# Taking the last 64 tokens of two batches through the first attention together, with tail outputs on 128x32 tiles

## The chip, the cores and the metric

The kernel runs on one core of one Trainium2 chip. The metric is the device time of one execution in microseconds (us), the median of several runs. A core has a matrix engine (PE, with its weight loads shown as PEld), a vector engine (DVE), a scalar engine (ACT), GpSimd (POOL) and a sync engine (SP) that issues DMAs. Each works through its own list of instructions in order; semaphores tie the lists together. Matmul results land in PSUM, which has eight banks of 512 fp32 columns on 128 partitions, and only DVE and ACT copy them out. DMAs issued from POOL, SP and ACT all move data between device memory and the core's SBUF.

## The reference

There are 8 batches of 576 tokens. The first stage is an attention with 8 heads of width 64, whose keys and values are averaged over groups of 8 tokens, so each head has 72 keys:

```python
k_p = k.reshape(B, H, Sp, pool, D).mean(axis=3)
v_p = v.reshape(B, H, Sp, pool, D).mean(axis=3)
scores = scale * np.matmul(q, k_p.transpose(0, 1, 3, 2))
attn = np.exp(scores - max); attn = attn / (attn.sum(-1) + 1e-09)
x = np.matmul(attn, v_p)          # heads side by side: B x S x 512
```

The second stage is a causal attention of width 64 in each of 4 experts; a gate keeps the best two experts of each token and weighs their outputs:

```python
logits = x @ w_gate               # top 2 of 4, softmax over the two
for e in range(E):
    q = x @ wq[e]; k = x @ wk[e]; v = x @ wv[e]
    a = softmax(causal(scale * (q @ k.transpose(0, 2, 1))))
    ye = a @ v @ wo[e]
    out += weight_of_expert_e * ye
```

## The kernel before, in words

576 tokens are four blocks of 128 and a tail of 64. The four blocks are the main part of a batch (512 columns). The tails of an even batch and the odd one after it share one block of 128: `place(b, 4)` is block 4 of a tile that holds both batches, and `half(b)` says which 64 partitions belong to which.

Nothing in the kernel is scheduled by the compiler. One long string, `SEQ`, lists all steps as tokens, and a loop at the end issues them one by one, so that the instructions of each engine stand in the string's order. A token reads: name, arguments, batch, then `@` and PSUM bank, then `d` for a copy on DVE instead of ACT, or `p` where a store is issued by a token of its own. `S12:3@4` is step S with arguments 1 and 2 for batch 3 into banks 4 and 5. Tokens with a capital letter are matmul groups on PE (H are idle matmuls at the start); the small letter of the same name is what empties the bank.

For each batch the steps are:

- `L`: loads of q (four quarters of 144 KB), k and v (576 KB each), issued on POOL's queue in the string's order and cast to bf16 on the way. q, k and v each have three buffers.
- `PK`, `kc`, `kt`: pool the keys and turn them; `PV`, `vc`: pool the values; `u`: turn q in 32x32 blocks.
- `E` and `e`: scores of the first attention and their exponential (`Es`, `es`). The argument is the head group 0 or 1 for the main part, and 2 for the tail of both groups.
- `D`, `d`, `x`: sums over the keys, then a logarithm and an exponential that give the reciprocals (`Dn`, `dn`, `dx`); `O`, `o`: outputs times reciprocals into the tile xT (`Ov`, `ov`). Again 2 is the tail.
- `P`, `p`: projections to the experts' queries and keys, `P_t` for the tail; `V`, `v`: values and gate logits; `g`: the gate.
- `S`, `s`, `a`: scores of the second attention, their exponential, the causal mask on POOL. `S03` is the tail's block against itself.
- `B`, then `bz`, `bg`, `b`: outputs of the second attention and their scaling. The last argument is the part: 0 and 1 for two blocks each, 2 for the tails of both batches (`B02`, `B12`: experts 0 and 1, and 2 and 3).
- `T`, `t` or `F`: the transpose before the last projection, through PE or by a DMA of SP; `Y`, `y`: last projection and copy, `z`: the store. `Y4` is the block of both tails, `ya` and `yb` the two halves of its copy in the last batch.

PE sees its 128x128 array in different shapes: E works on strips of 32 rows and 128 columns, S on 64 rows, the groups PK, PV, D and O on columns of 32, `B02` and `B12` on columns of 64, everything else on the whole array. Nearly all matmuls are issued by one helper, `mm` at line 226, so a view by line shows them all as L226; they are told apart by the tiles that they read.

The steps that the change touches are `Es`, `es` (line 336), `heads`, `Dn`, `part`, `Ov`, `ov` (lines 373 and 382), `P`, `p`, `Sb`, `sb` (lines 491 and 497), `am` and `Bv`, and the whole of `SEQ`. The second attention of a batch needs its tail's queries early: every score tile but the first reaches to token 576.

Of the kernel before, what the change touches and what calls it, by code (L numbers as in the profile page):

```python
# [8 lines left out]
FP32 = mybir.dt.float32  # L9
# [14 lines left out]
def kernel(  # L24
# [36 lines left out]
    LONG = (0,)  # L61
    HALF = TPP // 2
# [23 lines left out]
    etas = bufs(2, [KR, H, S], BF16, "eta")  # L86
    rzas = bufs(2, [128, 2, S], FP32, "rza")
# [4 lines left out]
    qks = bufs(2, [128, 2, NEP, SPAD], BF16, "qk")  # L92
# [6 lines left out]
    warm = const.tile([128, 512], BF16, name="warm")  # L99
    ident = const.tile([128, 128], BF16, name="ident")  # L100
    diff = const.tile([128, 128], FP32, name="diff")
# [151 lines left out]


# [56 lines left out]

    def four(pairs):
        return [pairs[0], pairs[0] + 1, pairs[1], pairs[1] + 1]

    def Es(b, pairs, g):
        banks = four(pairs)
        for j, cols, o in pieces(b, g):
            for par in range(2):
                for i in range(4):
                    rows = slice(32 * i, 32 * i + 32)  # L320
                    mm(psum[:, banks[i], o : o + cols.stop - cols.start],
                       kpTs[b % 2][rows, 2 * j + par].rearrange("p c j -> p (c j)"),
                       qTs[b % 2][rows, j, cols, par], start=(par == 0), stop=(par == 1))

    def es(b, pairs, dve, g, half):
# [4 lines left out]
        if len(got) == 2:  # L330
            dst = etas[b % 2][:, :, cols].rearrange(by, g=2)[:, 2 * half : 2 * half + 2]
# [4 lines left out]
        nc.scalar.activation(out=dst, in_=src, func=EXP, scale=ATT_EXP_SCALE)  # L336

    def heads(b, g, cols):
        for i in range(4):
            yield i, 4 * g + i, etas[b % 2][:, 4 * g + i, cols]  # L340
# [7 lines left out]
    def part(t, b, g):  # L348
        got = pieces(b, g)
# [12 lines left out]
    def Ov(b, bank, g, t):  # L362
        got = pieces(b, g)
# [107 lines left out]
    def Sb(b, bank, ep, ti):  # L471

        off = 0
        for i in range(NEP) if ti == 3 else [ep]:
            for c, c0, c1 in STILES[ti]:
                k0 = 128 * c - (64 if c == 4 and b % 2 else 0)
                for e in range(2):
                    r0 = e * HD
                    mm(psum[:, bank + e, off : off + c1 - c0],
                       qks[b % 2][r0 : r0 + HD, 1, i, k0 : k0 + 128],  # L480
                       qks[b % 2][r0 : r0 + HD, 0, i, c0:c1])
                off += c1 - c0

    def sb(b, bank, dve, ep, ti):
# [4 lines left out]
        if ti == 3:  # L489
            for e in range(2):  # L490
                nc.scalar.activation(
                    out=et[half(b), :, e, eo : eo + n],
                    in_=psum[half(b), bank + e, 0 : 2 * n].rearrange("p (a n) -> p a n", a=NEP),
# [8 lines left out]
    def am(b, ep, ti):  # L502
        et = etbs[b % 2]
        if ti == 3:
            blk = et[half(b), :, :, EOFF[4] : EOFF[4] + 64]
            nc.gpsimd.affine_select(
                out=blk, in_=blk, pattern=[[0, NEP], [0, 2], [1, 64]], compare_op=ISGE,
                fill=0.0, base=0, channel_multiplier=-1,
            )
# [108 lines left out]
    def z(b, c, queue):  # L618
# [16 lines left out]
        u00:0 r1:0d w1:0 u01:0 PK0:0@0 W0:0 kc0:0 PK1:0@0 W1:0 kt0:0d kc1:0 u10:0 L_k:1 E0:0@24 H1:0@1 u11:0 H1:0@0  # L635
        H1:0@0 H1:0@0 e00:0 kt1:0 e01:0 c1:0d E1:0@02 e11:0 H1:0@6 H1:0@6 H1:0@4 H1:0@5 e10:0 E2:0@46 PV:0@2 e20:0
        L_q3:1 e21:0 D2:0@3 D0:0@6 H1:0@7 D1:0@7 vc:0 O20:0@2 O01:0@4 d0:0 O00:0@6 c0:0d O11:0@5 x0:0 d1:0 x1:0 d2:0
        O10:0@0 H1:0@1 H1:0@1 c3:0 o00:0 H1:0@7 o01:0 L_q2:1 H1:0@1 o10:0 X0:0@6 o11:0 X1:0 X2:0 X3:0 c2:0 x2:0 o20:0
        P_k1:0@2 P_k0:0@3 P_t0:0@5 PK:1@4 p_k1:0 p_k0:0 W3:0 h0:0d L_q1:1 N:0 L_q0:1 W2:0 p_t0:0d S00:0@2 H1:0@6 H1:0@5
        S02:0@6 kc:1 L_v:1 S03:0@4 s00:0 S01:0@0 s02:0 H1:0@2 kt:1d s03:0 u1:1 H1:0@3 u0:1 E1:1@46 s01:0 L_k:2 E0:1@02  # L640
        c4:0d e10:1 e01:1 V2:0@4 v2:0d L_q0:2 a00:0 e11:1 V1:0@5 V3:0@2 V0:0@4 v1:0d D1:1@5 L_q3:2 v3:0d v0:0d L_q1:2
        PV:1@3 a02:0 e00:1 E2:1@06 D0:1@4 d1:1 L_q2:2 g0:0 vc:1d x1:1 H1:0@5 O10:1@5 o10:1 L_v:2 O11:1@3 d0:1 g1:0 g2:0
        o11:1 e20:1 x0:1 O01:1@2 O00:1@4 S12:0@0 B01:0@5 o01:1 e21:1 D2:1@3 s12:0 d2:1 PK:2@6 a01:0 g3:0 O20:1@7 o00:1
        bz01:0 S10:0@0 L_k:3 g4:0 x2:1 g5:0 g6:0 S11:0@2 P_q0:1@4 kc:2 g7:0 o20:1 s10:0 g8:0 P_q1:1@6 kt:2d L_q0:3 a12:0
        p_q0:1d V0:1@7 L_q3:3 s11:0 u1:2 p_q1:1 a11:0 P_t0:1@4 g9:0 bg01:0 L_q2:4 v0:1d a03:0 E1:2@02 p_t0:1 L_q1:3
        b01:0 u0:2 e10:2 V2:1@6 v2:1d a10:0 P_k0:1@7 p_k0:1d e11:2 E0:2@04 B11:0@6 B10:0@2 L_q2:3 L_k:4 B00:0@7 bz10:0
        e01:2 e00:2 bz11:0 PV:2@3 bz00:0 bg11:0 D1:2@4 b11:0 bg00:0 bg10:0 d1:2 P_k1:1@5 b00:0 vc:2d E2:2@06 b10:0
        D0:2@4 x1:2 e21:2 L_v:3 O11:2@3 L_q0:4 O10:2@2 p_k1:1d PK:3@6 d0:2 o11:2 O01:2@7 S03:1@4 kc:3 e20:2 x0:2 o01:2
        S01:1@0 L_q1:4 o10:2 V3:1@3 L_q3:4 s03:1 s01:1 V4:1@6 v3:1 S10:1@4 O00:2@7 S00:1@0 v4:1d s10:1 S11:1@2 s00:1
        V1:1@6 T00:0@4 L_v:4 o00:2 P_q0:2@5 s11:1 kt:3d t00:0d v1:1d S02:1@0 a03:1 u0:3 s02:1 p_q0:2d S12:1@6 P_q1:2@4  # L650
        E0:3@02 g1:1 g2:1 g3:1 g0:1 a00:1 V2:2@5 s12:1 u1:3 g4:1 g5:1 p_q1:2d P_k1:2@6 e01:3 v2:2d E2:3@24 g6:1 P_k0:2@7
        L_q0:5 e20:3 L_q3:5 a02:1 p_k1:2d e21:3 T10:0@6 t10:0d g7:1 g8:1 E1:3@24 p_k0:2d B12:1@6 g9:1 e00:3 PK:4@0 e11:3
        PV:3@1 a10:1 bz12:1 bg12:1 S00:2@4 kc:4 e10:3 a12:1 b12:1 vc:3d B02:1@7 D1:3@6 bz02:1 u0:4 D0:3@0 B01:1@1
        T11:0@2 a11:1 W4:0 V3:2@3 s00:2 bz01:1 D2:2@4 bg02:1 d0:3 D2:3@0 t11:0d O01:3@5 bg01:1 O11:3@2 d1:3 L_k:5 x0:3
        d2:3 O10:3@6 b02:1 x1:3 b01:1 v3:2d d2:2 B10:1@1 o01:3 kt:4 T01:0@7 t01:0 L_q1:5 V1:2@0 v1:2 V0:2@3 v0:2 O00:3@5
        PV:4@4 x2:2 o10:3 O20:2@0 o11:3 o00:3 L_q2:5 u1:4 E0:4@26 vc:4 x2:3 L_q2:6 P_k1:3@5 P_q1:3@4 bz10:1 bg10:1 e01:4
        o20:2 g1:2 b10:1 p_q1:3d E1:4@06 e00:4 Y1:0@2 p_k1:3d y1:0dp L_v:5 V2:3@4 v2:3d Y3:0@3 L_q1:6 e11:4 Y2:0@5 g2:2
        P_t0:2@2 y3:0dp e10:4 y2:0p L_k:6 a01:1 p_t0:2d g0:2 E2:4@06 D0:4@4 e21:4 O20:3@5 L_q0:6 d0:4 o20:3 g3:2 O01:4@3
        PK:5@2 D1:4@6 L_v:6 S12:2@4 P_k0:3@7 e20:4 x0:4 kc:5 s12:2 S10:2@0 d1:4 o01:4 S11:2@2 S02:2@4 s10:2 p_k0:3d
        V4:3@6 kt:5d s11:2 B11:1@7 T02:1@0 P_q0:3@1 s02:2 T12:1@2 u1:5 p_q0:3 t02:1d bz11:1 V1:3@3 u0:5 P_t0:3@0 x1:4  # L660
        L_q3:7 p_t0:3 O00:4@4 v4:3d bg11:1 v1:3d L_q3:6 g4:2 D2:4@1 L_q0:7 L_q2:7 PV:5@6 b11:1 O10:4@7 t12:1d a00:2
        O11:4@5 d2:4 o00:4 vc:5 E2:5@02 e21:5 V3:3@4 g5:2 o10:4 S03:2@6 o11:4 S01:2@2 e20:5 s03:2 s01:2 S01:3@0 v3:3d
        B00:1@5 bz00:1 T10:1@6 x2:4 g6:2 t10:1d P_k0:4@4 a01:2 bg00:1 s01:3 E0:5@26 b00:1 e01:5 V0:3@5 T11:1@0 p_k0:4d
        a12:2 t11:1d P_k1:4@4 e00:5 E1:5@06 e11:5 v0:3d B00:2@5 bz00:2 p_k1:4d Y4:1@2 e10:5 g7:2 P_q0:4@3 T01:1@4 g8:2
        y4:1dp g1:3 a02:2 g9:2 S11:3@6 PK:6@2 p_q0:4d bg00:2 b00:2 O20:4@0 kc:6 g2:3 O01:5@1 t01:1 s11:3 a01:3 D0:5@3
        d0:5 PV:6@4 L_v:7 O11:5@5 o20:4 O00:5@6 g3:3 g4:3 g0:3 D1:5@2 x0:5 vc:6d D2:5@0 zs2:0 d1:5 a10:2 O10:5@3 o01:5
# [121 lines left out]
```

## Time and profile before

| | us |
|---|---|
| median of three runs | 156.86 (156.32 to 157.36) |
| the profiled execution, its own time | 154.86 |
| its span, first to last instruction | 153.1 |
| PE busy | 140.8 (92%) |
| ACT busy | 131.0 (86%) |
| DVE busy | 116.0 (76%) |
| POOL busy | 91.5 (60%) |

The granted PE clock is 0.984 of full speed over the span. Busy times of a stage say little by themselves: the engines work on several batches at once, and PE's matmuls are pipelined. Read where each engine waits, and for what. In the rows of the profile a line gives start and length in us, engine, source line, operation, what is written and read, the shape, and how often; in square brackets stands how long the engine was idle before it and what ended that.

### The profile page before, as it was taken

The numbers are of one execution on the slowest core, as the hardware profiler recorded it, in microseconds if no ns is written. First come the engines' busy times: TensorE is split into PE (matmuls) and PEld (weight loads), VectorE is DVE, ScalarE is ACT, GpSimd is POOL, SyncE is SP. The second block draws the span as 40 slices with busy tenths as digits, with TensorE's granted clock in tenths as the row PEclk, the third lists the DMA queues.
The fourth block names the chain that finished last, engine by engine and source line by source line (L and its number), as shares of the span: only waits on it lengthen the run. The fifth ranks groups of instructions, "written<-read, shape, count | busy, mean of one in ns | idle before, by whom it ended". The sixth has DMA issues, their size and how long they took to land.

```text
span 153.1 us, 5376 instructions
## 1 busy us (share of the span) xinstructions
PE 140.8 (92%) x2118; PEld 75.7 (49%) x2118; DVE 116.0 (76%) x341; ACT 131.0 (86%) x235; POOL 91.5 (60%) x211
## 2 busy tenths in 40 slices
PE   6778996999999999999999999999999999999920
PEld 2223452555553555556545666744545656656410
DVE  1871785698899599889879979897785866798440
ACT  3359759998999899999999999999999999887910
POOL 6995449689776896983469544440752655682000
PEclk9999999999999999999999999999999999999985
DMA  4999999999999999999999993166250027899976
GB/s 126 235 188 181 183 177 182 182 180 184 181 182 183 180 183 184 180 185 246 182 178 117 234 153 43 39 72 180 92 197 2 4 49 72 279 354 370 345 285 196
DMA packets 68282, 26.67 MB, mean 174 GB/s; under 512 B 62112, under 2 KB 63392, under 8 KB 68256
## 3 DMA queue, kind: packets, MB, share of 16 engines
q0 software_dynamic: 56928, 14.72, 96.8%
q1 hardware_dynamic: 10960, 10.88, 23.5%
q10 hardware_dynamic: 368, 0.72, 1.6%
q8 instruction: 16, 0.26, 0.7%
q14 instruction: 10, 0.08, 0.1%
HBM read 30.42 MB, written 9.44 MB: 260 GB/s over the span
## 4 chain that ended last, share of the span: by engine, by line
PE 70%; DMA 12%; ACT 8%; POOL 3%; DVE 2%; issue 1%; DVEq 0%; POOLq 0%
PE psum L226 69%; DMA qraw<-in_q_dram 7%; DMA vraw<-in_v_dram 5%; ACT etb L497 3%; ACT eta L336 3%; POOL kraw L133 2%; PE psum L235 1%; ACT rza L359 1%; POOL qraw L133 1%; ACT rza L355 1%; DVE qT L303 1%; ACT vaug L217 0%; DVE otail L567 0%; DVE kf L283 0%; DVE ofin L217 0%
## 5 line engine op out<-in xcount | busy, mean ns | idle before, releaser
L497 ACT ACTIVATE etb<-psum 128x1024 bf16<-128x1024 f32 x48 | 47.0, 1030 | 1.4 <-PE psum L226 1.1
L336 ACT ACTIVATE eta<-psum 96x1024 bf16<-96x1024 f32 (+1 forms) x48 | 36.3, 807 | 3.5 <-PE psum L226 3.2
L514 POOL TENSOR_SCALAR_AFFINE_SELECT etb<-etb 128x256 bf16<-128x256 bf16 x64 | 24.9, 409 | 13.5 <-ACT etb L497 13.4
L133 POOL DMA_DIRECT2D qraw<-in_q_dram x30 | 20.0, 674 | 5.3 <-DMA vraw<-in_v_dram 3.6
L382 DVE TENSOR_TENSOR xT<-psum,rza 128x512 bf16<-128x512 f32 x32 | 20.5, 681 | 1.6 <-ACT rza L359 0.8
L226 PE MATMUL psum<-wvg,xT 128*128 128x260 bf16 x144 | 20.0, 274 | 0.4 <-ACT eta L336 0.4
L226 PE MATMUL psum<-xT,wqp 128*128 128x64 bf16 (+1 forms) x128 | 19.5, 286 | 0.0
L226 PE MATMUL psum<-wop,oT 128*128 128x512 bf16 (+1 forms) x74 | 19.2, 374 | 0.3 <-DVE oT L217 0.3
L226 PE MATMUL psum<-xT,wkp 128*128 128x512 bf16 (+1 forms) x128 | 19.3, 286 | 0.0
L226 PEld LDWEIGHTS <-etb 128*128 128x128 bf16 (+1 forms) x480 | 14.9, 102 | 7.3 <-issue 4.5
L217 DVE CAST qk<-psum 128x512 bf16<-128x512 f32 (+2 forms) x26 | 16.3, 638 | 2.6 <-PE psum L226 2.3
L226 PE MATMUL psum<-vaug,etb 128*128 128x65 bf16 (+1 forms) x480 | 17.4, 195 | 0.0
L226 PE MATMUL psum<-qk 64*128 64x64 bf16 (+4 forms) x192 | 16.0, 276 | 0.2
L226 PEld LDWEIGHTS <-xT 128*128 128x128 bf16 x144 | 12.9, 97 | 6.3 <-issue 2.7
L217 DVE COPY ofin<-psum 128x512 f32<-128x512 f32 (+1 forms) x18 | 11.9, 669 | 3.4 <-PE psum L226 3.3
L303 DVE STREAM_TRANSPOSE qT<-qraw 128x576 f32<-128x576 f32 (+1 forms) x18 | 13.4, 753 | 0.9 <-DMA qraw<-in_q_dram 0.8
L133 POOL DMA_DIRECT2D kraw<-in_k_dram x11 | 11.5, 1051 | 4.3 <-DMA kraw<-in_k_dram 3.4
L567 DVE TENSOR_TENSOR osc<-psum,gt 128x256 bf16<-128x256 f32 x32 | 13.4, 421 | 0.6
L226 PE MATMUL psum<-qT,kpT 32*128 32x64 bf16 (+1 forms) x256 | 12.4, 289 | 1.4 <-DVE qT L303 1.3
L217 ACT COPY ofin<-psum 128x512 f32<-128x512 f32 (+1 forms) x19 | 10.4, 579 | 3.6 <-PE psum L226 3.3
L226 PE MATMUL psum<-eta,vp 96*32 96x64 bf16 (+1 forms) x256 | 12.9, 287 | 0.0
L359 ACT ACTIVATE rza<-rza 128x512 f32<-128x512 f32 (+1 forms) x24 | 12.6, 529 | 0.1
(81 smaller groups left out, 216.8 us busy)
## 6 DMA issues: line engine op xcount, KB each, us to landing
out_dram<-ofin SPq DMA_DIRECT2D x32, 256.0 KB, 3.2
vraw<-in_v_dram POOLq DMA_DIRECT2D x8, 576.0 KB, 11.8
qraw<-in_q_dram POOLq DMA_DIRECT2D x30, 144.0 KB, 9.8
kraw<-in_k_dram POOLq DMA_DIRECT2D x7, 576.0 KB, 10.7
out_dram<-ofin SPq DMA_DIRECT2D x7, 128.0 KB, 3.6
xT<-in_q_dram ACTq DMA_DIRECT2D x2, 288.0 KB, 4.6
xT<-in_k_dram SPq DMA_DIRECT2D x2, 192.0 KB, 4.9
kraw<-in_k_dram POOLq DMA_DIRECT2D x4, 96.0 KB, 5.1
```

What stands on the lines that cost most here:

```text
L133: nc.gpsimd.dma_start(out=dst, in_=src)
L217: (nc.vector.tensor_copy if dve else nc.scalar.copy)(out=out, in_=in_)
L226: nc.tensor.matmul(out=out, lhsT=lhsT, rhs=rhs, start=start, stop=stop)
L235: nc.tensor.transpose(out=out[s], in_=in_[:, s], identity=ident[0:n, 0:n])
L303: nc.vector.transpose(out=dst.rearrange("p (a s n) -> p a n s", s=32, n=n)[:, :, own], in_=src.rearrange("p (a n d) -> p a n d", n=n, d=32 ...
L336: nc.scalar.activation(out=dst, in_=src, func=EXP, scale=ATT_EXP_SCALE)
L355: nc.scalar.activation(out=rz, in_=z, func=LN)
L359: nc.scalar.activation(out=rz, in_=rz, func=EXP, scale=-1.0)
L382: nc.vector.tensor_tensor(out=xT[:, 2 * got[0][0] + t : 2 * got[-1][0] + t + 1 : 2, m + got[0][1].start : m + got[0][1].stop], in0=psum[:, ...
L497: nc.scalar.activation(out=et[:, ep, :, eo : eo + n], in_=psum[:, bank : bank + 2, 0:n], func=EXP, scale=MOE_EXP_SCALE,)
L514: nc.gpsimd.affine_select(out=blk, in_=blk, pattern=[[0, 2], [1, 128]], compare_op=ISGE, fill=0.0, base=0, channel_multiplier=-1,)
L567: nc.vector.tensor_tensor(out=osc(b, ep, part).rearrange("p c (e d) -> p e c d", e=2), in0=o[:, :, :, 0:HD], in1=gt.to_broadcast([128, 2, ...
```

## The change

From batch 2 on, the tails of an even batch and of the odd batch after it pass the first attention together, when the odd batch is at its turn: `PAIRED = (3, 5, 7)`. The tokens `E2`, `e2`, `D2`, `d2`, `x2`, `O2`, `o2`, `P_t`, `p_t`, `S03`, `s03` and `a03` of batches 2, 4 and 6 are gone, and those of 3, 5 and 7 work on both tails. Batches 0 and 1 keep their own. The tails' exponentials and reciprocals get tiles of their own; the tile for the idle matmuls and one for constants move into them.

`sb` for the tails makes one call per batch over both experts of a pair of banks in place of two. `Bv` for the tails writes pieces of 32 tokens in place of 64, with twice as many matmuls on 128x32 tiles. The whole string is ordered anew: PE has 2206 matmuls in place of 2118, ACT 204 instructions in place of 235, DVE 346 in place of 341. Some copies change between ACT and DVE, banks are given out anew, the loads stand in another order, and the store of the last block (`zs4:7`) becomes a token at the very end.

```diff
+    PAIRED = (3, 5, 7)
-    etas = bufs(2, [KR, H, S], BF16, "eta")
-    rzas = bufs(2, [128, 2, S], FP32, "rza")
+    etas = bufs(2, [KR, H, MAIN], BF16, "eta")
+    eta_ends = bufs(2, [128, H, 2 * TAIL], BF16, "etaT")
+    etaTs = [t[0:KR] for t in eta_ends]
+    rzas = bufs(2, [128, 2, MAIN], FP32, "rza")
+    rzaT = const.tile([128, 2, 2 * TAIL], FP32, name="rzaT")
...
+    def tails(b):
+        return (b - 1, b) if b in PAIRED else (b,)
+    def ends(b):
+        n = len(tails(b))
+        return [(j, bb, TAIL * m, TAIL * (n * j + m)) for j in range(2) for m, bb in enumerate(tails(b))]
...
     def Dn(b, bank, g):
+        if g == 2 and b in PAIRED:
+            for h in range(H):
+                mm(psum[32 * (h % 4) : 32 * (h % 4) + 32, bank, 2 * TAIL * (h // 4) : 2 * TAIL * (h // 4) + 2 * TAIL],
+                   onesd[:, :], etaTs[b // 2 % 2][:, h, :])
+            return
...
-        cols, n = (tcols(b), TAIL) if nm == "t" else (mcols(b), MAIN)
+        cols, n = (tail_cols(b), TAIL * len(tails(b))) if nm == "t" else (mcols(b), MAIN)
...
-            for e in range(2):
+            for m, bb in enumerate(tails(b)):
                 nc.scalar.activation(
-                    out=et[half(b), :, e, eo : eo + n],
-                    in_=psum[half(b), bank + e, 0 : 2 * n].rearrange("p (a n) -> p a n", a=NEP),
+                    out=etbs[bb % 2][half(bb), :, :, eo : eo + n].rearrange("p a e n -> p e a n"),
+                    in_=psum[half(bb), bank : bank + 2, 2 * n * m : 2 * n * m + 2 * n].rearrange(
+                        "p e (a n) -> p e a n", a=NEP),
                     func=EXP, scale=MOE_EXP_SCALE,
                 )
...
                     for h in range(2):
-                        mm(av(b, bank, part)[64 * h : 64 * h + 64, e, 0, :],
-                           etbs[h][:, ep, e, col : col + TAIL],
-                           vaugs[b // 2 % 2][:, place(h, c), 2 * ep + e, :], start=(c == 0), stop=(c == NTC - 1))
+                        for x in range(0, TAIL, 32):
+                            mm(av(b, bank, part)[64 * h + x : 64 * h + x + 32, e, 0, :],
+                               etbs[h][:, ep, e, col + x : col + x + 32],
+                               vaugs[b // 2 % 2][:, place(h, c), 2 * ep + e, :], start=(c == 0), stop=(c == NTC - 1))
...
-        Y2:7@2 B12:7@0 bz12:7 B02:7@4 bg12:7 bz02:7 b12:7 T12:7@5 bg02:7 b02:7 T02:7@0 t12:7d t02:7d Y4:7@4 zs3:6 y2:6p
-        y1:7p y0:7p y3:7p y2:7p zs2:6 zs1:7 zs0:7 ya4:7 yb4:7d zs3:7 zs2:7
+        zs1:4 T01:7@5 y0:7dp a03:7 t01:7d T11:7@2 t11:7d B02:7@1 zs0:4 bz02:7 bg02:7 B12:7@0 bz12:7 Y3:7@2 y2:6p b02:7
+        Y2:7@5 T02:7@1 bg12:7 b12:7 y1:6p t02:7d y1:7p y3:7p zs0:6 zs3:6 zs2:6 zs1:6 zs0:7 zs1:7 y2:7p T12:7@4 zs3:7
+        t12:7d Y4:7@0 ya4:7dp yb4:7p zs2:7 zs4:7
```

The loads of batches 3 to 5 stand in the string in these orders, with a quarter of q as q and a digit for the batch:

```
before: k3 q3 q3 q4 q3 q3 k4 v3 q4 q4 q4 v4 q5 q5 wo k5 q5 q5 q6 v5
after:  k3 q3 q3 q3 q3 q4 q4 q4 q4 k4 wo v3 k5 v4 q5 q5 q5 q5 v5
```

More of the change, by code (lines that the diff above doesn't have):

```diff
@@ L91 @@
     etbs = bufs(2, [128, NEP, 2, ECOLS], BF16, "etb")
-    qks = bufs(2, [128, 2, NEP, SPAD], BF16, "qk")
+    qk_all = const.tile([128, 2, 2, NEP, SPAD], BF16, name="qk")
+    qks = [qk_all[:, i] for i in range(2)]
     vaugs = bufs(2, [128, NPC, E, HD + 1], BF16, "vaug")
@@ L362, in Ov @@
     def Ov(b, bank, g, t):
+        if g == 2 and b in PAIRED:
+            for h in range(H):
+                for u in range(2):
+                    for j, bb, m, _ in ends(b):
+                        if j == h // 4:
+                            o = 4 * TAIL * j + 2 * TAIL * u + m
+                            mm(psum[32 * (h % 4) : 32 * (h % 4) + 32, bank, o : o + TAIL],
+                               vps[bb % 2][:, h, u::2], etaTs[b // 2 % 2][:, h, m : m + TAIL])
+            return
         got = pieces(b, g)
@@ L504, in am @@
         if ti == 3:
[L505 to L509, printed above, removed]
+            for bb in tails(b):
+                blk = etbs[bb % 2][half(bb), :, :, EOFF[4] : EOFF[4] + 64]
+                nc.gpsimd.affine_select(
+                    out=blk, in_=blk, pattern=[[0, NEP], [0, 2], [1, 64]], compare_op=ISGE,
+                    fill=0.0, base=0, channel_multiplier=-1,
+                )
             return
@@ L649 @@
[L649 to L653, printed above, removed]
```

175 lines of the change are left out of this document (96 added, 79 removed).

## The prediction

> **What bounds the kernel now.** I read the page first, for which engine is full and where.
>
> ```profile
> span 153.1 us, 5376 instructions
> PE 140.8 (92%) x2118; PEld 75.7 (49%) x2118; DVE 116.0 (76%) x341; ACT 131.0 (86%) x235; POOL 91.5 (60%) x211
> PE   6778996999999999999999999999999999999920
> PEclk9999999999999999999999999999999999999985
> DMA  4999999999999999999999993166250027899976
> ```
>
> PE is at nine tenths from the eighth slice to the last but two. The DMA engines are full through the first 24 slices (some 95 us), then free, then full again at the end with the output. ACT is nearly as full as PE, so which of the two bounds has to be settled. For that I read the sums by stretch:
>
> ```profile
> core 0: us, PE busy (x) PEld busy (x) DVE busy (x) ACT busy (x) POOL busy (x), PEclk, DMA share, GB/s
> 25.00:60.00 35.00, 34.32 (x569) 18.09 (x565) 29.70 (x83) 33.30 (x61) 28.38 (x58) 1.00 1.80 182
> 60.00:100.00 40.00, 40.00 (x690) 23.12 (x688) 34.98 (x102) 39.27 (x73) 24.67 (x58) 1.00 1.36 155
> 100.00:144.50 44.50, 44.39 (x584) 25.08 (x584) 34.82 (x111) 41.53 (x76) 20.74 (x69) 1.00 0.57 165
> ```
>
> Both look full, and a busy PE here may be matmuls whose modelled ends overlap a wait. So I go to the timeline of PE alone and take differences of starts, which no modelled end can blur:
>
> ```profile
> 52.20 0.63 PE L226 MATMUL psum<-qT,kpT 32*128 32x512 bf16 x8
> 52.76 0.51 PE L226 MATMUL psum<-vaug,etb 128*64 128x65 bf16 x20
> 53.20 0.52 PE L226 MATMUL psum<-kraw,poolk 96*32 96x128 bf16 x24
> ...
> 62.54 0.60 PE L226 MATMUL psum<-wop,oT 128*128 128x512 bf16 x2
> 62.98 0.61 PE L226 MATMUL psum<-wvg,xT 128*128 128x260 bf16 x4
> 63.43 1.02 PE L226 MATMUL psum<-wop,oT 128*128 128x512 bf16 x4
> 64.29 0.40 PE L226 MATMUL psum<-xT,wqp 128*128 128x64 bf16 x8
> ...
> 65.30 0.51 PE L226 MATMUL psum<-eta,vp 96*32 96x64 bf16 x20
> 65.64 0.51 PE L226 MATMUL psum<-kraw,poolk 96*32 96x128 bf16 x24
> ```
>
> Two matmuls of 512 columns take 62.98 - 62.54 = 0.44 us, so 0.22 each; four of 260 columns 0.45, so 0.11 each; four more of 512 columns 0.86, again 0.22. That is columns streamed one after the other with nothing between. Eight matmuls on 32-row strips run four at a time, 8 x 0.22 / 4 = 0.43, but the next group starts 0.56 later: 0.13 us go where the shape of the array tile changes. So in the middle PE does not wait; its time is columns streamed plus about 0.13 us for each change of tile shape. What is won there must come out of columns or changes.
>
> At the head PE waits for data, and at the end for the last tail:
>
> ```profile
> 23.71 0.78 DVE L303 STREAM_TRANSPOSE qT<-qraw 128x576 f32<-128x576 f32 x1 [0.84 <-DMA qraw<-in_q_dram]
> 24.55 1.30 PE L226 MATMUL psum<-qT,kpT 32*128 32x512 bf16 x16 [0.88 <-DVE qT L303]
> 26.29 0.94 PE L226 MATMUL psum<-wvg,xT 128*128 128x260 bf16 x7 [0.43 <-ACT eta L336]
> ```
>
> So batch 1 cannot start before its queries land (about 23.6), whatever stands ahead of it; from 24.55 on the time is PE's order.
>
> **The change, part by part.** Everything is a difference against the profiled execution's 154.86 us, whose span is 153.1.
>
> *1. PE's own work.* I counted matmuls and changes of tile shape in the two program orders. The merged P_t of two batches streams 16 x 128 columns in place of 32 x 64. From 64.29, eight 64-column matmuls take about 8 x 0.03 = 0.23 (the row's 0.40 includes the drain of the last), so 0.93 a pair; 16 x 0.22 / 4 = 0.88 after. Three pairs: -0.15 us with the merged denominators. Scores and outputs of the tails keep their count. The eight tail outputs (B02, B12) go from 20 matmuls on 128x64 tiles to 40 on 128x32. From 52.76 to 53.20 the old form takes 0.44 with its change of shape, so 0.31. The new form was never run with 128 rows, but the nearest row is at 65.30: 20 matmuls with 32-column tiles, four of them of 512 columns, take 0.34; 0.22 of it is those four, which leaves 0.12 for 16, four at a time in 0.03. Forty then take 0.30: equal. Bounds: 0.30, and 0.60 if only two ran at a time (+2.4 us over eight); I take 0.30. What the new form does win is neighbours: D, O, PK and PV have the same shape, so no change falls between them. By my count the changes after batch 1's first scores fall from 110 to 108 (of 126 and 122 in all): 2 x 0.13 = -0.26. Changes out of the old 128x64 shape were the dearer ones, for which I add -0.2. Sum -0.6 us, from -0.9 to +1.8.
>
> [...]
>
> *2. ACT.* Merging takes off twelve short exponentials and gives six of double length, and the masks' sources (s03) become one call per batch in place of two.
>
> ```profile
> L336 ACT ACTIVATE eta<-psum 96x1024 bf16<-96x1024 f32 x32 | 31.0, 1023 | 3.0 <-PE psum L226 2.7
> L336 ACT ACTIVATE eta<-psum 96x256 bf16<-96x256 f32 x16 | 5.5, 376 | 0.5 <-PE psum L226 0.5
> L359 ACT ACTIVATE rza<-rza 128x512 f32<-128x512 f32 x16 | 10.2, 635 | 0.1
> L359 ACT ACTIVATE rza<-rza 128x128 f32<-128x128 f32 x8 | 2.6, 319 | 0.0
> L491 ACT ACTIVATE etb<-psum 64x128 bf16<-64x128 f32 x16 | 3.5, 266 | 0.5 <-PE psum L226 0.4
> ```
>
> The 96x512 form stands between its two rows: 0.376 + 0.647 x 256 / 768 = 0.59, so 12 x 0.376 - 6 x 0.59 = 0.97 off. Reciprocals: 0.42 for 256 columns by the same line, 6 x 0.319 - 3 x 0.42 = 0.65 off, and the logarithms before them about as much (0.6). Masks: 16 x 0.266 - 8 x 0.37 = 1.3 off. That is 3.5 us; copies that the new order hands from ACT to DVE take some 2.7 more (counted over the tokens), and DVE gains about 1.1 on balance. Value for the end: 0, since PE's starts above show no wait on ACT in the middle. Bounds: 0 and -5; the latter is a rival.
>
> *3. The loads.* Their order moves, and this costs.
>
> ```profile
> DMA packets 22045, 5.83 MB, mean 182 GB/s; under 512 B 21795, under 2 KB 22038, under 8 KB 22038
> ...
> 60.30 1.19 POOL L133 DMA_DIRECT2D vraw<-in_v_dram  x1 [0.54 <-PE psum L226]
> vraw<-in_v_dram POOLq DMA_DIRECT2D x1, 576.0 KB, 10.8
> 71.62 0.59 PE L226 MATMUL psum<-vraw,poolv 96*32 96x512 bf16 x4
> ```
>
> The first row is the stretch from 28 to 60 us: 5.83 MB in 32 us, so 576 KB need 3.2 and a quarter of q 0.8. The others are batch 5's values: issued at 60.30, landed 10.8 later at 71.1, first used at 71.62, half a microsecond of margin. In the new order one quarter of q less stands ahead of them, so they land about 70.3; but by my sum of streamed columns and changes PE has 2.0 us less to do before it reaches that group, and gets there at 69.6. It waits 0.7. Earlier, batch 4's keys now stand behind three more quarters of q, and the wait would be absorbed in this one. At the head nothing is gained: q of batch 1 is still behind the same 576 KB of k. Value +0.7, bounds 0 and +1.5: the upper one if the stretch from 25 to 37 us, where the row at 26.29 shows PE on ACT's heels, passes its delay on.
>
> *4. The last tail.*
>
> ```profile
> 143.00 1.59 PE L226 MATMUL psum<-wop,oT 128*128 128x512 bf16 x6
> 144.51 0.82 PE L226 MATMUL psum<-vaug,etb 128*64 128x65 bf16 x40
> 145.89 0.23 PE L235 MATMUL psum<-ident,otail 128*128 128x128 bf16 x1 [0.55 <-DVE otail L567]
> 146.28 0.23 PE L235 MATMUL psum<-ident,otail 128*128 128x128 bf16 x1 [0.17 <-DVE otail L567]
> 146.83 0.61 PE L226 MATMUL psum<-wop,oT 128*128 128x256 bf16 x4 [0.32 <-DVE oT L217]
> ...
> 147.48 0.42 DVE L217 COPY ofin<-psum 128x256 f32<-128x256 f32 x1 [0.71 <-PE psum L226]
> 147.97 0.48 SPq L622 DMA_DIRECT2D out_dram<-ofin  x1
> 148.51 1.07 SPq L626 DMA_DIRECT2D out_dram<-ofin  x2
> ```
>
> Before, the two tail outputs stand last, and PE idles 0.55 + 0.17 + 0.32 and more while DVE scales them. In the new order two projections (Y3:7 and Y2:7, each 2 x 0.22) stand between the tail outputs and their transposes. They cover 0.87 of a wait that is at least 1.04; what stays is the hand-over of the last transpose to its copy and on to Y4. I take -0.8; bounds -1.0 and -0.4.
>
> *5. The last stores.* Before, two stores of 256 KB are issued behind the last one's first half, at 148.51 and 0.54 after that; the end at 153.1 is theirs. In the new order the last projection's store is the last, so those two are ahead of it if the queue has come that far. That is 148.51 + 0.54 - 147.97 = 1.1 us less after the last copy; the smaller last store (two halves of 128 KB on two queues) may add 0.1. I take -1.2; bounds -1.6, and +0.5 if the queue is behind.
>
> Sum: -0.6 + 0 + 0.7 - 0.8 - 1.2 = -1.9 us. The profiled execution would take 154.86 - 1.9 = 153.0. The median of the runs shown, 156.86, stands 2.0 above the profiled execution, so the median forecast is **155.0 us**.
>
> **The rivals.**
>
> *ACT is the bound after all.* For it: 39.27 of 40.00 and 41.53 of 44.50 us busy, and a busy PE may be waiting. [...] Against it: the starts 62.54, 62.98, 63.43 and 64.29 leave no room. If it holds, part 2 pays up to 5 of its 6.2 us, of which I allow 2.5 beyond the sum: 152.5.
>
> *The store queue is behind.* The order moves the stores; nine of them then follow each other at the very end, and at 0.54 us each they need 4.9 us. If the queue reaches them 1.5 us late, part 5 turns from -1.2 to +0.3: 156.5, no change. For it: the DMA row is at nine tenths there. Against: the same number of stores leaves the queue over the same stretch before.
>
> *The merged tails starve PE* (the other side). Each merged tail is one serial chain: scores, exponentials, denominators, logarithm, reciprocal, output, multiplication, projection, copy. From a denominator to its output the reciprocal alone is 0.42 and the logarithm as much, 0.84; in the new order about 1.0 us of other PE work lies between them, and each chain occurs three times with two such joints more (multiplication to projection, copy to scores). If every joint is short by 0.6 us, nine joints cost 5.4: 160.4. It decides from 0.4 us a joint on, where 3.6 us would make the kernel over 1% slower. Against: the covers that I counted at the other joints are 1.2 us and more.
>
> *Weight loads follow each other in the tail outputs.* [...] By the trace the bound is two at a time, which was 0.60 in part 1, +2.4 us in all: 157.4. Against: the 16 matmuls at 65.30 have 16 different stationary slices and take 0.12.
>
> **How the numbers follow.** Forecast 53% (154.0 to 156.2), ACT the bound 7%, store queue 20%, starved tails 15%, weight loads 5%. A difference of 1% (1.6 us) is about what a measurement of this kernel can tell from no change. The forecast's own spread reaches over -1%: about 0.43 of its 0.53 is faster, the rest the same. Faster 0.43 + 0.07 = 0.50; the same 0.10 + 0.20 + 0.03 = 0.33; slower 0.17. The range runs from 152.8 (ACT freed in part) to 158.2 (the starved tails from their point of decision, and the weight loads).
>
> **What would show it.** Part 1: a tail output group followed 0.30 to 0.45 us later by the next group; more than 0.6 is the weight-load rival. Part 2: ACT's busy sum near 125 us while PE stays at its full digits. Part 3: batch 5's value pooling waiting for its DMA, and less than a microsecond in all such waits. Parts 4 and 5: under a microsecond of idle PE between the last tail output and Y4, and no store issued after Y4's. The prediction is wrong if PE shows idle time in the middle, or if stores are still being issued two microseconds after the last copy.

## The result, and the profile after

The changed kernel takes **164.27 us** (median of four runs, 162.26 to 164.99); the kernel before took 157.11 in the same comparison (156.32 to 158.71). The ratio is 1.0515, 95% interval 1.0414 to 1.0616. The forecast was 155.0 with a range to 158.2: wrong in sign, and 9.3 us off.

The page of the changed kernel (an execution of 164.99 us, span 163.1) already says where to look. It is the longest of its four runs, and the profiled execution of the kernel before (154.86) is a short one, so the difference of these two, which is taken apart below, is 10.0 us where the medians differ by 7.2.

```profile
span 163.1 us, 5500 instructions
...
PE 145.6 (89%) x2206; PEld 76.6 (47%) x2206; DVE 117.2 (72%) x346; ACT 128.7 (79%) x204; POOL 91.4 (56%) x211
...
PE   6886997999999995999999955999999999999940
...
PEclk9999997799999999999999995599999999999996
DMA  4999999999999999999399990016052224799995
...
q8 instruction: 17, 0.28, 0.7%
```

PE's digits fall to 5 in slice 16 (61 to 65 us) and in slices 24 and 25 (94 to 102 us), and the granted clock falls twice, to 7 and to 5; before, both rows stood at nines in these slices, but for the head. PE has 88 pairs of a weight load and a matmul more than before (2206 against 2118). The last row is the queue that brings instructions; it returns below. The timeline of PE at the two places (start, duration, operation, and in brackets the idle time ahead of it with what ended it):

```profile
59.09 0.85 PE L231 MATMUL psum<-vaug,etb 128*32 128x65 bf16 x80
...
62.94 0.36 PE L231 MATMUL psum<-etaT,vp 96*32 96x64 bf16 x19
65.36 0.24 PE L231 MATMUL psum<-etaT,vp 96*32 96x64 bf16 x5 [2.06 <-issue]
...
94.16 0.49 PE L231 MATMUL psum<-vaug,etb 128*32 128x65 bf16 x40
94.48 0.45 PE L231 MATMUL psum<-etaT,vp 96*32 96x64 bf16 x29
...
95.51 0.53 PE L231 MATMUL psum<-kraw,poolk 96*32 96x128 bf16 x24
95.85 0.38 PE L231 MATMUL psum<-eta,onesd 96*32 96x512 bf16 x1
99.59 1.04 PE L231 MATMUL psum<-eta,onesd 96*32 96x512 bf16 x7 [3.35 <-issue]
```

Both stalls lie **inside** a group of equal matmuls: after 19 of the 32 of O20 of batch 3, and after the first of the four of D1 of batch 6. Their operands were there, or the first ones could not have run. "issue" means that the profile shows nothing that PE waited for. PE's waits summed by what ended them (total, times, longest):

```profile
PE psum L231 <- issue: 5.4, 2, 3.4
PE psum L231 <- DMA vraw<-in_v_dram: 1.3, 1, 1.3
```

The clock, by stretches of 3.41 us on the grid on which it changes (PE busy is the second number, the granted clock the one before the DMA share):

```profile
23.40:26.81 3.41, 2.00 (x22) 0.56 (x19) 2.79 (x6) 3.39 (x5) 2.66 (x5) 1.00 1.89 185
26.81:30.22 3.41, 3.23 (x16) 2.20 (x15) 1.35 (x6) 2.86 (x4) 2.70 (x3) 0.50 1.81 178
...
95.08:98.49 3.41, 1.15 (x69) 0.73 (x63) 1.89 (x7) 1.07 (x2) 0.42 (x2) 1.00 1.04 113
98.49:105.31 6.82, 5.72 (x52) 3.49 (x52) 1.73 (x4) 2.86 (x5) 0.00 (x0) 0.50 0.01 2
```

At half clock two matmuls of 512 columns take 0.84 us (102.29 to 103.13), against 0.44 in the kernel before. If matmuls that keep PE busy for 3.23 us at half clock need half of that at full clock, the first stretch costs an estimated 1.6 us and the second, 5.72 busy, 2.9. The sixteen matmuls of 260 columns that start in the first stretch take 3.42 us (26.99 to 30.41); in the first experiment, at full clock, they take 1.89. The end, in the timeline of PE and DVE:

```profile
156.41 0.61 PE L231 MATMUL psum<-wop,oT 128*128 128x256 bf16 x4 [0.18 <-DVE oT L222]
...
157.06 0.42 DVE L222 COPY ofin<-psum 128x256 f32<-128x256 f32 x1 [0.57 <-PE psum L231]
```

and in that of SP, whose rows are stores:

```profile
144.16 14.30 SPq L672 DMA_DIRECT2D out_dram<-ofin  x20
158.56 0.74 SPq L668 DMA_DIRECT2D out_dram<-ofin  x1
```

PE itself has little idle time left ahead of its last group (0.18), but SP issues twenty stores on end for 14.3 us, and its half of the last block's store goes out 1.08 us after the copy has ended (157.48).

The difference of the two spans, 163.1 - 153.1 = 10.0 us, is then made up like this (batch 1's first scores start at 25.23, before at 24.55; Y4 of batch 7 at 156.41, before at 146.83):

| where | us |
|---|---|
| batch 1's first scores start later | +0.7 |
| half clock from 26.8 to 30.2 | +1.6 |
| stall in O20 of batch 3 (2.42 from start to start, less the work of 19 matmuls) | +2.3 |
| stall in D1 of batch 6 | +3.5 |
| half clock from 98.5 to 105.3 | +2.9 |
| from Y4's start to the end, 6.69 against 6.27 | +0.4 |
| what remains | -1.4 |

The last row is a remainder, not a measurement. Of it 0.9 us is seen: PE idled 1.04 us between the last tail outputs and Y4 before, and idles 0.18 there now. The other 0.5 has no measured cause. The first row, too, is partly chance: the run with part 4 alone, which has the head of the kernel before, starts these scores at 25.01.

### The profile page after: what moved, and what is told of

It reads as the page before. It is cut to its first block, busy times and chain, and to the rows that moved or that the text cites. A ratio compares the mean times of both kernels' runs of the same rounds, so it can differ in the third digit from the quotient of the medians.

```text
span 163.1 us, 5500 instructions
## 1 busy us (share of the span) xinstructions
PE 145.6 (89%) x2206; PEld 76.6 (47%) x2206; DVE 117.2 (72%) x346; ACT 128.7 (79%) x204; POOL 91.4 (56%) x211
## 4 chain that ended last, share of the span: by engine, by line
PE 67%; ACT 9%; DMA 8%; issue 6%; DVE 3%; POOL 3%; ACTq 0%; POOLq 0%; DVEq 0%
PE psum L231 65%; ACT etb L541 5%; DMA vraw<-in_v_dram 5%; DMA out_dram<-ofin 3%; POOL kraw L138 2%; PE psum L240 1%; DVE xT L421 1%; PE psum L219 1%; DVE ofin L222 1%; POOL qraw L138 1%; ACT rza L384 1%; ACT ofin L222 1%; ACT eta L357 1%; ACT vaug L222 0%; ACT rza L388 0%
## 5 line engine op out<-in xcount | busy, mean ns | idle before, releaser
L357 ACT ACTIVATE eta<-psum 96x1024 bf16<-96x1024 f32 x32 | 30.7, 1024 | 1.0 <-PE psum L231 0.9
L231 PEld LDWEIGHTS <-etb 128*32 128x32 bf16 (+1 forms) x640 | 16.7, 97 | 6.1 <-issue 2.7
L222 DVE CAST qk<-psum 128x512 bf16<-128x512 f32 (+1 forms) x22 | 14.4, 660 | 6.9 <-PE psum L231 5.8
L231 PE MATMUL psum<-xT,wkp 128*128 128x512 bf16 (+2 forms) x104 | 19.2, 321 | 0.0
L231 PE MATMUL psum<-xT,wqp 128*128 128x512 bf16 (+2 forms) x104 | 19.1, 321 | 0.0
L231 PE MATMUL psum<-vaug,etb 128*32 128x65 bf16 (+1 forms) x640 | 19.0, 196 | 0.0
L222 DVE CAST vaug<-psum 128x256 bf16<-128x256 f32 x31 | 13.0, 421 | 5.3 <-PE psum L231 5.1
L384 ACT ACTIVATE rza<-psum 128x512 f32<-128x512 f32 x16 | 9.3, 596 | 7.7 <-PE psum L231 7.7
L606 DVE RECIPROCAL rzb<-psum 128x4 f32<-128x4 f32 (+1 forms) x40 | 6.9, 174 | 9.6 <-PE psum L231 9.3
L460 POOL TENSOR_TENSOR ahead<-L 128x64 bf16<-128x64 f32 (+1 forms) x8 | 2.5, 308 | 19.7 <-DVE L L222 17.6
```

The source lines that it names most:

```text
L222: (nc.vector.tensor_copy if dve else nc.scalar.copy)(out=out, in_=in_)
L231: nc.tensor.matmul(out=out, lhsT=lhsT, rhs=rhs, start=start, stop=stop)
L384: nc.scalar.activation(out=rz, in_=z, func=LN)
L460: pool.tensor_sub(out=tmp("ahead", E, E), in0=other, in1=L.unsqueeze(3).to_broadcast([128, n, E, E]))
L606: nc.vector.reciprocal(out=rz, in_=o[:, :, :, HD : HD + 1])
```

## The experiments

**Theory T1, instruction supply.** PE's program is 4416 instructions and a few more, pairs of a weight load and a matmul behind four others. The queue of the last row brings 0.28 MB in 17 packets, 16 KB each; 4416 / 17 gives an estimate of 260 instructions to a packet. The stalls come before instruction 1730 and before 2754 (863 and 1375 matmuls have run), which is 1024 apart; from the packet at the first stall (63.15 us) to the one at the second (97.06) it is four packets, so by this estimate 256 instructions to each. The theory is that PE's instructions arrive in blocks of 256, with borders at 194, 450, 706 and so on. PE enters the block that ends at 1730 at about 59.4 us (33 matmuls into the pair at 59.09) and goes on at 65.4; the block that ends at 2754 at about 94.3, and goes on at 99.6. That gives 6.0 and 5.3 us from entering one block until the next is there. A block with less work than that leaves PE idle, and these hold 3.7 and 1.6 us: the doubled tail outputs take 8 ns a matmul (40 in the 0.32 us from 94.16 to 94.48), and the new order puts them next to O, PK and PV on the same 32-column tiles, which are as short.

**Rival R1**: the stalls are waits of the new order, on loads or engines. **Rival R2**: the 128x32 matmuls are slow themselves.

### The tail outputs back on 128x64

```diff
-                        for x in range(0, TAIL, 32):
-                            mm(av(b, bank, part)[64 * h + x : 64 * h + x + 32, e, 0, :],
-                               etbs[h][:, ep, e, col + x : col + x + 32], ...)
+                        mm(av(b, bank, part)[64 * h : 64 * h + 64, e, 0, :],
+                           etbs[h][:, ep, e, col : col + TAIL], ...)
```

> The changed kernel with one part undone: the tail outputs are 20 matmuls on 128x64 tiles again, 320 PE instructions fewer; order, merging and waits are as changed. Theory T1, instruction supply: PE's instructions arrive in blocks of 256, a block is there 5.3 to 6.0 us after PE has entered the one ahead of it, and a block with less PE work than that leaves PE idle. By the streamed columns the shortest blocks now last 5.8 us, so the stalls of 2.3 and 3.5 us near 63 and 96 us go, and with the second one the half-clock stretch (2.9 us); 8 groups of another tile shape cost 0.7. 164.3 - 8.7 + 0.7 = 156.3 us. Theory R1, the new order's waits: both stalls stay at the same groups, 164 to 165 us. Theory R2, the 128x32 matmuls are slow themselves: each tail output group takes 0.3 us less than with 32-wide tiles, 2.4 us in all, 161.9 us.

Measured: 157.37 us (155.75 to 159.75, ten runs), ratio to before 1.0068 (1.002 to 1.0116). PE's waits in this kernel:

```profile
PE psum L231 <- DMA vraw<-in_v_dram: 1.2, 2, 0.9
...
PE psum L231 <- issue: 0.5, 3, 0.2
```

and its clock, from the page:

```profile
PEclk9999999999999999999999999999999999999996
```

Of the 5.4 us of "issue" 0.5 is left, in pieces of 0.2, and this execution has no half clock before its end: 6.9 us are gone with 160 matmuls fewer for the same work (the ratio to the kernel before falls from 1.0515 to 1.0068). So far T1 holds. R1 falls, since the order is unchanged; R2 falls, since in the changed kernel the 40 matmuls at 94.16 are followed by the next group 0.32 us later. The time is 1.1 us above the 156.3 expected; what waits came in place of the stalls stands with part 3 of the prediction below.

### The same program, 114 places later

```diff
     def warm_up(n, bank, low):
         rows = slice(KR, 128) if low else slice(0, 128)
         for _ in range(n):
-            nc.tensor.matmul(out=psum[rows, bank, :], lhsT=warm[:, rows], rhs=warm[:], ...)
+            warmed[0] += 1
+            step = 128 if warmed[0] <= 19 else 512
+            for x in range(0, 512, step):
+                nc.tensor.matmul(out=psum[rows, bank, x : x + step], lhsT=warm[:, rows], rhs=warm[:, x : x + step], ...)
```

> The changed kernel with 19 of its warm-up matmuls of 512 columns at the head cut into four of 128 columns: the same columns, 114 PE instructions more, everything behind them is the same and only sits 114 places later in the program. T1: the block borders fall elsewhere. The stall near 96 us goes (shortest block there 5.5 us), the one near 63 us moves to the start of batch 3's third denominators (about 59.5 us) and is 1.0 to 1.9 us long; 164.3 - 8.7 + 1.4 = 157.0 us, to 160 if the clock falls after it. R1 and R2: no change, 164.3 us, the stalls at the same groups.

Measured: 158.08 us (157.37 to 159.68), ratio 1.0143 (1.009 to 1.0197). The timeline of PE at the stall:

```profile
60.71 0.29 PE L237 MATMUL psum<-etaT,onesd 96*32 96x128 bf16 x6
62.68 0.23 PE L237 MATMUL psum<-etaT,onesd 96*32 96x128 bf16 x2 [1.68 <-issue]
```

and two stretches of the clock's grid:

```profile
59.50:62.91 3.41, 1.67 (x23) 0.59 (x20) 1.85 (x5) 1.95 (x3) 3.32 (x6) 1.00 2.06 175
62.91:66.32 3.41, 3.41 (x81) 2.09 (x72) 2.45 (x4) 2.04 (x5) 1.65 (x4) 0.50 1.99 175
```

To cut nineteen idle matmuls at the head into four pieces each, which changes no work, wins 6.2 us (164.27 to 158.08; in ratios to the kernel before, 1.0515 to 1.0143). The border at 1730 falls on what was instruction 1616, behind the sixth of the eight matmuls of D2 of batch 3; PE stops after exactly six, for 1.68 us. The stall near 96 us is gone, as expected. Half clock follows the one that is left and costs an estimated 3.41 / 2 = 1.7 us. Neither R1 nor R2 gives any change here.

### The narrow tail outputs in the order before

The kernel before with the first diff reversed: `B02` and `B12` on 32 columns, nothing else.

> The kernel before with one part of the change alone: its tail outputs as 40 matmuls on 128x32 tiles, 320 PE instructions more; order and waits as before. T1: blocks of 3.5 and 3.2 us arise, so PE stalls inside or next to B02 of batch 1 (near 55 us, 2.1 us) and inside E2 of batch 6 (near 100 us, 2.4 us): 157.1 - 0.6 + 4.5 = 161.0 us, and up to 3 us more for each stall that the half clock follows. R1: 156.5 us, the 0.6 us that the tile shapes give. R2: 159.5 us, each of the eight groups 0.3 us longer, with no stall elsewhere.

Measured: 158.43 us (156.73 to 159.7), ratio 1.0102 (0.9977 to 1.0228), which alone decides little. The timeline decides:

```profile
55.19 0.45 PE L226 MATMUL psum<-vaug,etb 128*32 128x65 bf16 x33
57.53 0.24 PE L226 MATMUL psum<-vaug,etb 128*32 128x65 bf16 x7 [1.89 <-issue]
...
98.52 0.30 PE L226 MATMUL psum<-eta,vp 96*32 96x64 bf16 x16
98.65 0.39 PE L226 MATMUL psum<-eta,onesd 96*32 96x512 bf16 x4
98.86 0.51 PE L226 MATMUL psum<-vaug,etb 128*32 128x65 bf16 x40
...
101.90 0.30 PE L226 MATMUL psum<-qT,kpT 32*128 32x64 bf16 x16
102.13 0.40 PE L226 MATMUL psum<-eta,onesd 96*32 96x512 bf16 x4
```

The first stall is there, in B02 of batch 1 after 33 of 40, which is instruction 1474, a border again; expected were 2.1 us near 55. The second, expected in E2 of batch 6, is **not**: the block from about 98.6 to 102.0, whose end falls in the row at 101.90, holds 3.4 us and PE runs through. So 5.3 to 6 us is not a fixed time. What differs at 98 us is that the loads are over (DMA share 0.04 from 98 to 103). This asked for a run of its own.

### No loads from batch 4 on

All `L` tokens of batches 4 to 7 are taken out of the order of the changed kernel; everything else stays. These batches then compute on what their buffers still hold, so the run is good for timing alone.

> The changed kernel without the loads of batches 4 to 7 (those batches compute on what the three buffers still hold, so the output of these batches is not the reference's); PE's instructions and their places are the same, and from about 46 us on the DMA engines are nearly idle. What sets the time until a block of instructions is there? If it waits behind the loads (T1 with contention), it is there about 3 us after PE enters the one ahead: no stall in O20 of batch 3 (block of 3.8 us), and one of at most 1.5 us in D1 of batch 6 (block of 1.5 us); 164.3 - 2.3 - 2.0 and, if no half clock follows, - 2.9 = 157 to 160 us. If the time is fixed at 5.3 to 6.0 us, both stalls stay at 2.3 and 3.5 us, 163 to 164 us. If the stalls were waits on loaded data (R1), they vanish wholly.

Measured: 157.77 us (two runs). PE's timeline:

```profile
93.27 0.38 PE L231 MATMUL psum<-eta,onesd 96*32 96x512 bf16 x1
95.12 0.61 PE L231 MATMUL psum<-eta,onesd 96*32 96x512 bf16 x7 [1.48 <-issue]
```

and the instruction queue's row (packets, MB, time as a share of sixteen engines) for the stretch from 91 to 96 us:

```profile
q8 instruction: 1, 0.02, 1.7%
```

The stall in O20 is gone, although its block is as short as before; the one in D1, at the same instruction 2754, has shrunk from 3.35 to 1.48 us. From entering the block (about 91.7) to going on it is now 3.4 us. The packet itself is short: 1.7% of sixteen engines for 5 us is 1.4 us. In the changed kernel the packet of the first stall comes late: from 59.35 us, when PE enters the block, to 63.1 the queue has no row at all, and from 63.1 to 65.4 it has this one:

```profile
q8 instruction: 1, 0.02, 2.6%
```

That is 1.0 us of one engine. So under load it is the start of the packet that is late: 3.8 and 2.8 us after PE enters the block at the two stalls (63.15 and 97.06 us), 0.8 us without loads (92.5), and at most 0.7 us in the run before this one, where the loads had ended by themselves (PE enters at about 98.6, and from 99.27 to 102.68 the DMA engines move nothing). The profile counts this queue on the same sixteen engines that carry the loads; that the packet waits in these engines, and not in the memory behind them, is not shown.

### Warm-up matmuls ahead of batch 1

```diff
-        s02:0 E1:1@46 e11:1 ...
+        s02:0 H4:0@0 E1:1@46 e11:1 ...
```

> The changed kernel with four warm-up matmuls between the last score of batch 0 ahead of batch 1 (S02 of batch 0) and batch 1's first scores, where PE is idle from 24.1 to 25.2 us. If idle time costs the clock, the half-clock stretch from 26.8 to 30.2 us goes and with it 2.0 us: 162.3 us, with the two later stalls as they are. If that stretch has another cause, or ACT was the bound there (it works without a break from 25.9 to 29.7 us), nothing changes: 164.3 us.

Measured: 164.82 us (163.81 to 165.16), ratio 1.0537 (1.0444 to 1.0629): nothing won. The early half clock did go, and PE reached O20 of batch 3 at 61.38 in place of 62.94. That the warm-up matmuls did it is not shown: the first two experiments, the no-loads run and the one with few stores below have the changed kernel's order there, without warm-ups, and no half clock near 27 us. This is the no-loads run, as busy ahead of it as the changed kernel was (2.01 against 2.00 us):

```profile
22.95:26.36 3.41, 2.01 (x28) 0.51 (x26) 3.13 (x6) 3.16 (x5) 2.63 (x6) 1.00 1.93 178
26.36:29.77 3.41, 2.94 (x46) 1.95 (x42) 1.79 (x8) 3.41 (x5) 2.86 (x3) 1.00 1.83 183
```

What was won was given back at O20, as PE's timeline shows:

```profile
64.09 0.37 PE L231 MATMUL psum<-etaT,vp 96*32 96x64 bf16 x15 [2.40 <-issue]
...
100.14 0.29 PE L231 MATMUL psum<-kraw,poolk 96*32 96x128 bf16 x3 [3.81 <-issue]
```

and the clock's grid:

```profile
60.79:64.20 3.41, 1.01 (x60) 0.77 (x56) 1.78 (x3) 2.06 (x5) 2.85 (x7) 1.00 1.81 181
64.20:67.61 3.41, 3.19 (x40) 1.39 (x39) 1.98 (x3) 1.62 (x2) 1.80 (x3) 0.50 1.70 216
```

The stalls stand eight instructions earlier (after 15 of O20, and in PK of batch 7 after 21 of 24), as the eight that were added demand. The first is longer than the changed kernel's, and it lies inside one stretch of the grid: PE is busy for 1.01 of its 3.41 us, and half clock follows. In the changed kernel the same stall lay across a border of the grid, with PE busy for 2.37 and 2.41, and the clock stayed:

```profile
60.94:64.36 3.42, 2.37 (x67) 1.36 (x68) 3.13 (x6) 3.40 (x6) 2.82 (x5) 1.00 1.81 182
64.36:67.77 3.41, 2.41 (x45) 1.51 (x45) 1.94 (x4) 1.64 (x3) 2.71 (x5) 1.00 1.83 180
```

The expectation had the stalls in the right places, 0.3 and 0.5 us too short, and overlooked that half clock could come back elsewhere: gone at 26.8 us, it stood at 64.20.

### What the end is worth

Two runs ask what parts 4 and 5 could have won. The first takes stores away (from the kernel with 128x64 tail outputs):

```diff
-        ... y3:7p zs0:6 zs3:6 zs2:6 zs1:6 zs0:7 zs1:7 y2:7p T12:7@4 zs3:7
+        ... y3:7p y2:7p T12:7@4
```

> The changed kernel with 128x64 tail outputs, without seven of the last nine ordinary stores (four blocks of batch 6 and blocks 0, 1 and 3 of batch 7 are not written except batch 6's tail). It asks what sets the end behind Y4 of batch 7, 6.4 us in the run with all stores, where the last nine stores land 0.6 to 0.7 us apart. If the end is the backlog of stores, it falls to about 5.0 us (copy 0.5, issue 0.6, landing 2.6, and 0.9 to the end). If the last block's own copy, issue and landing set it, it stays at 6.2 to 6.4 us.

Measured: 154.29 us (153.74 to 154.83), ratio 0.9938 (0.9895 to 0.9981); span 152.5 with Y4 of batch 7 at 147.22. From there to the end it is 5.3 us in place of 6.6: the backlog of stores is worth 1.3 us. The second does part 4 alone, in the kernel before:

```diff
-        T01:7@2 Y0:7@3 t11:7d t01:7d Y3:7@7 y3:6p
-        Y2:7@2 B12:7@0 bz12:7 B02:7@4 bg12:7 bz02:7 b12:7 T12:7@5 bg02:7 b02:7 T02:7@0 t12:7d
+        T01:7@2 Y0:7@3 t11:7d t01:7d y3:6p
+        B12:7@7 bz12:7 B02:7@4 bg12:7 bz02:7 b12:7 bg02:7 b02:7 Y3:7@0 Y2:7@2 T12:7@5 T02:7@7 t12:7d
```

> The kernel before with part 4 alone: its two tail outputs of the last batches stand ahead of Y3 and Y2 of batch 7, so these two projections lie between the tail outputs and their transposes. If PE's last work sets the end (part 4 as predicted): idle PE there falls from 1.4 to about 0.5 us and the time by 0.8, 155.5 us. If the backlog of stores sets it: PE's Y4 starts 0.8 us earlier all the same, but the stretch from there to the end grows from 6.3 to 6.8 us or more, and the time stays within 0.3 us of before, 156.0 us.

Measured: 155.45 us against 155.76 in the same comparison, ratio 1.0001 (0.9951 to 1.005). PE's timeline:

```profile
146.12 0.61 PE L226 MATMUL psum<-wop,oT 128*128 128x256 bf16 x4 [0.38 <-DVE oT L217]
```

and SP's:

```profile
142.24 5.28 SPq L626 DMA_DIRECT2D out_dram<-ofin  x8
147.64 0.48 SPq L622 DMA_DIRECT2D out_dram<-ofin  x1
148.18 1.92 SPq L626 DMA_DIRECT2D out_dram<-ofin  x2
```

PE's idle time between the tail outputs and Y4 falls from 1.04 to 0.38 us, and from batch 1's first scores (25.01) to Y4 PE needs 121.1 us in place of 122.3; but from Y4 to the end it is 7.3 in place of 6.3. The eight stores ahead take 5.28 / 8 = 0.66 us each. The last block's store does go out sooner (147.64, before 147.97), but issuing the two behind it takes 1.92 us in place of 1.07, so they are out at 150.10, before at 149.58: 125.1 and 125.0 us after batch 1's first scores. PE's gain is there, and off the path.

### A mixture

The tail outputs on 64 columns for batches 1 and 3, on 32 for 5 and 7 (`n = 64 if b < 4 else 32`), the four warm-ups, and `PV:5@7 vc:5d` moved behind `O10:4`.

> The changed kernel with three edits: tail outputs on 128x64 tiles for batches 1 and 3 and on 128x32 for 5 and 7, four warm-up matmuls ahead of batch 1's first scores, and batch 5's value pooling three groups later, behind O10 of batch 4. T1: no block under 5.6 us while the loads run, so no stall over 0.3 us in the middle; the short blocks of batches 5 and 7 lie behind the loads, where the DMA engines are free, and cost nothing. Against the run with 128x64 tiles throughout (157.4): no wait for batch 5's values (-1.0), fewer changes of tile shape (-0.3), no half clock at the head (0 to -0.5): 156.0 us, level with before or just ahead. If short blocks cost the same without loads, stalls of 2 us or more show near 120 us: 158 us.

Measured: 157.56 us (156.73 to 159.54), ratio 1.0143 (1.0093 to 1.0193). As T1 wants, no stall over 0.2 us in the middle and no half clock in the profiled execution, though batches 5 and 7 keep their dense blocks; they lie behind the loads. The rest of the expectation failed. PE's waits:

```profile
PE psum L231 <- issue: 0.7, 4, 0.2
...
PE psum L231 <- DMA vraw<-in_v_dram: 0.3, 1, 0.3
```

The wait for batch 5's values is not there (the 0.3 are batch 0's), but it was not in the sixth experiment either, which has the old place of that group; and in the timeline a transpose into the bank of that group now waits for its copy:

```profile
75.75 0.22 PE L240 MATMUL psum<-ident,otail 128*128 128x128 bf16 x1 [0.47 <-DVE vp L222]
```

and from Y4 (148.48) to the end (155.5) it is 7.0 us. No run beat the kernel before with all its work done, and none of them points to one that would.

## Why the prediction was wrong, step by step

**Part 1 is the step that failed**, in its sentence "Forty then take 0.30: equal." The duration was right: 0.32 us from the start of the 40 matmuls at 94.16 to the next group. What had no price was that 40 matmuls are twice the instructions. The part counted columns, changes of shape and neighbours; the rivals were about the array, the engines, the stores and the chain of a tail. The neighbours that it counted as a gain, equal shapes side by side, are what made blocks of 3.7 and 1.6 us. The missing term is the two stalls, 5.8 us, and the half clock behind the second, 2.9. Undoing that one part, with the order kept, took 6.9 us off. The half clock at 26.8 (1.6) had no term either. The new order no longer puts two warm-up matmuls ahead of batch 1's first scores, but the four runs named above have that head and kept the full clock there, so in this execution it was bad luck more than a cost of the change.

**The condition for being wrong was the right one**: "if PE shows idle time in the middle". So was the sign of the rival that starved PE, with 160.4 us, but not its mechanism: joints between the steps of a tail are not where PE waits. The upper end of the range, 158.2, was also set below that rival's own point of decision, which is 155.0 + 3.6 = 158.6; the measured time lies above both.

**Part 4's gain** came on PE: 0.18 us idle ahead of Y4 in place of 1.04, where -0.8 was forecast. But it is worth nothing: alone, it left the time where it was (ratio 1.0001). **Part 1's gain** (-0.6) is not shown. Of its -0.2 for the dearer changes out of 128x64, the kernel before shows this much: its groups of 20 at 52.76, 54.40, 94.74 and 95.74 us take 0.44 to 0.46 from start to start, by an estimate 0.28 of it columns (20 x 65 columns, two matmuls at a time), which leaves 0.16 to 0.18 for the change, against 0.13 on the strips. That the remainder of the account, -1.4, equals the two forecasts together is no proof: 0.5 of it is left for part 1, and two executions of kernels that are equal up to the last stores differ by 1.6.

**Part 2** took 0 as ACT's value, which held: no long wait of PE on ACT in the changed kernel (the longest are 0.5 on `kraw` and 0.4 on `eta`, both at the head). The durations of ACT's instructions, added up one by one, fell from 151.6 to 144.9 us, close to the 6.2 that the part worked out; the busy time, in which instructions that overlap count once, fell only from 131.0 to 128.7. So the part was right in its count and wrong in its sign, a busy sum near 125.

**Part 3** said 0.7 us for batch 5's values. In the changed kernel PE does not wait there (the 1.3 us on `vraw` are batch 0's). Without the stalls, in the first experiment, it waits 0.9, and 1.0 more at 37.3 us for queries that landed late; in the sixth, whose order is the same up to the last stores, it waits 0 and 0.7. So the new order of the loads does cost something, between 0.7 and 1.9 us in these two executions.

**Part 5** was wrong, and its rival (the store queue is behind, 20%) right: 1.08 us late at the last issue, where 1.5 was the rival's figure. In place of -1.2 the end cost +0.4. With 128x64 tail outputs, taking seven stores away shortened the end by 1.3.

**Without the instruction supply** the forecast's terms that reach the end were part 3's +0.7 and, with 128x64 tiles, the 0.15 of part 1 that the merging gives. The first experiment measured +1.1 us over before (157.37 against 156.27). What else the order costs or wins is below what single profiles tell: the kernels of the first and the sixth experiment are equal up to the last stores, and from batch 1's scores to Y4 they took 123.9 and 122.3 us, nearly all of the difference being the waits for loads just named. The kernel before took 122.3.

## What to carry to other kernels

Count instructions per stretch of time, not only time per instruction: here, where matmuls of 8 ns stood together, blocks of 256 instructions held 3.7 and 1.6 us of work, and their successors took 5.3 to 6.3 us to arrive while loads ran, and 3.4 without them. The sign was a stall inside a group of equal instructions, put down to nothing; an edit that only moved the program by 114 places told it from a wait. And before work is taken off the last engine, see whether the stores behind it would leave any sooner.

## What the runs showed of the hardware

**PE's instructions came in blocks of 256, over a DMA queue.** Every stall over 1 us that the profiles put down to nothing stands at instruction 194 + 256 k of PE's program (1474, 1730 or 2754), in five kernels, and the instruction queue moved 16 KB to a packet (0.28 MB in 17). From entering a block to having the next it took 5.3 to 6.3 us while loads ran, 3.4 us without them.

**The granted clock changed on a grid of 3.41 us.** In the changed kernel it changes at 26.81, 30.22, 98.49 and 105.31 us, which are 1, 20 and 2 steps of 3.41 apart. From full clock, half clock followed stretches in which PE was busy for 1.01, 1.15, 1.41, 1.52 and 1.67 of 3.41 us, and once 2.00; it did not follow 1.83, 1.85, 1.94 and 2.01 in the heads of other runs, nor 2.37 and 2.41. PE's busy time is modelled, so no sharper line can be drawn from it. The stall in O20 brought one stretch of half clock in the warm-up run, by estimate 1.6 us (half of the 3.19 that PE was busy in it), and none in the changed kernel; the grids of the two runs have borders at 64.20 and 64.36 us.

**Three gaps between landed stores stand behind fetched blocks.** Seen and not tested: while the stores leave at the end, their landings mostly follow each other by 0.6 to 0.7 us, but by 2.8 and 1.9 us just after the blocks that the changed kernel fetches at 146.6 and 156.6 us, and by 1.9 after the one of the kernel before at 139.9. That the fetch caused the gaps is not shown.
